# Splitting -log f into two float32r halves, and joining y to the next chunk's scores, from the third block on

## The chip, the cores and the metric

The kernel runs on one core of a Trainium2 chip. Times are device microseconds (us), given as the median of several runs.

## The reference, cut to what matters

```python
f = 1.0 / (1.0 + np.exp(-f_logit))               # q, k, v, f_logit: (4, 8, 768, 48)
for t in range(S):
    state = f[:, :, t, :, None] * state + np.einsum('bhd,bhe->bhde', k[:, :, t], v[:, :, t])
    y[:, :, t] = np.einsum('bhd,bhde->bhe', q[:, :, t], state)
# y is reshaped to x: 3072 tokens x 384
h = x @ w_in                                     # 384 -> 2048
sp = np.maximum(h, 0.0) + np.log1p(np.exp(-np.abs(h)))
out = (h * erf(sp)) @ w_out                      # 2048 -> 384
```

All arithmetic is float32. The first part is a recurrence over 768 steps, the second a pair of large products around an elementwise function.

## The kernel before

The recurrence is done in 24 chunks of 128 tokens, three chunks to a block, eight blocks. A chunk `g` goes through four stages, and each needs the one before it:

- `stage_d`: `tri` times -log f gives the running sums `ps_d`. ScalarE makes two exponentials of them, `dp` and `kd`. VectorE makes `qd`, GpSimd multiplies into `kd`.
- `stage_t`: TensorE transposes `qd` and `kd`, the copies are `qT` and `kT`.
- `stage_s`: scores `sc` on TensorE, masked into `A` on VectorE, then `dS` and the state `Mbd`.
- `stage_y`: `y` from `A`, v and the state, ScalarE copies it into `xT`.

```python
def prepare(blk, j0, j1):                 # -log f of a whole block, in place
    ...
    nc.vector.tensor_scalar(out=lt, in0=lt, scalar1=LOGIT_MIN, scalar2=None, op0=ALU.max)
    use_exp_ln()
    nc.scalar.activation(out=lt, in_=lt, func=AF.Exp, scale=-1.0)
    nc.scalar.activation(out=lt, in_=lt, func=AF.Ln, bias=1.0)

def stage_d(g):
    ...
    nc.tensor.matmul(ps, lhsT=tri[:], rhs=lts[blk][:, j, :], start=True, stop=True)
    ...    # dp and kd on ScalarE, qd on VectorE, kd on GpSimd
```

These stages are laid by hand between the large products. A *slot* is one large product, of 384 columns: two passes of 0.32 us, so about 0.64 us. Iteration `it` runs the hidden products of block `it` and the projections of block `it-2`, 96 slots together (48 in the first two iterations, which have no projection). The chunk stages of block `it+1` are dropped in at evenly spaced slots, and with them go activation steps of finished groups, clamps, and, up to about 146 us, unpacking of the weights on VectorE.

```python
todo = deque(stages(blk) if blk < n_blocks else [])
at = [int(3 + (n - 13) / max(1, len(todo)) * i) for i in range(len(todo))]
for s, _ in enumerate(slots(it)):         # one large product
    ...                                   # due weight steps
    if at and s == at[0]:
        at.pop(0)
        f, g = todo.popleft()
        f(g)
        ...
    ...                                   # step: is an activation step due at s?
    if step and not 66 <= s < 72:
        act_step()
    if it + 2 < n_blocks and s == (16 if it < 2 else n // 2):
        prepare(it + 2, 0, CPB)
```

The position of a stage thus depends on how many stages there are: `at` spaces them evenly. The order in which this loop emits instructions is the order in which ScalarE and VectorE run them in the traces looked at below. The large products take turns in a pool of two buffers (`hps` and `ops`); VectorE copies `hps` out to `Hg` from the third block on, ScalarE copies `ops` out to `osb`.

## Time and profile before

| | before |
|---|---|
| time, median of 4 (range) | 648.12 us (648.04 to 648.44) |
| span of the profiled execution | 646.4 us |
| hidden products of block 0 / 3 / 7 begin at | 32.19 / 208.86 / 515.28 us |
| busy in that span: TensorE, VectorE, ScalarE | 630.7, 474.6, 510.0 us |

Read the third row as marks: where a block's hidden products begin tells how late the kernel is at that point, and two kernels can be compared mark by mark. (Blocks are counted from 0: block 3 is the fourth.) The lines that carry the reading are shown in the prediction.

### The profile page before, as it was taken

The page shows a single profiled execution, that of the slowest core. Times are in us where ns is not written, and L with a number is a line of the kernel's source. Part 1 is how long each engine was busy: PE and PEld are TensorE (multiplying, and loading weights), DVE is VectorE, ACT ScalarE, POOL GpSimd, SP SyncE. Part 2 cuts the span into 40 slices and gives each one's busy share as a digit, 9 for nine tenths or more (in the row PEclk, how much of TensorE's full clock was granted, in tenths as well). Part 3 has the DMA queues.
Part 4 walks back from the last instruction along what each step waited for, and adds up shares of the span by engine and source line. Part 5 has one row for each costly group of instructions (what it writes and reads, how often), then busy time and mean ns, then how long its engine had stood idle before and what let it go on. Part 6 is the DMA issues. An engine that isn't in the chain of part 4 may idle for free.

```text
span 646.4 us, 9360 instructions
## 1 busy us (share of the span) xinstructions
PE 630.7 (98%) x3815; PEld 393.8 (61%) x3815; DVE 474.6 (73%) x440; ACT 510.0 (79%) x459; POOL 59.1 (9%) x61
## 2 busy tenths in 40 slices
PE   8899999999999999999999999999999999999995
PEld 6756666665656666656656666666666655555553
DVE  4798889997777886678657687668765686577761
ACT  5446667679899888797898978978787899799971
POOL 0112101120110010201210002201020000000000
PEclk9999999999999999999999999999999999999999
DMA  9996872310113120221203211020001000000001
GB/s 192 252 269 149 220 204 50 75 24 14 37 37 74 25 38 13 62 50 25 38 13 76 45 28 24 13 75 1 1 0 38 1 0 1 37 1 0 37 1 41
DMA packets 120689, 36.90 MB, mean 57 GB/s; under 512 B 112448, under 2 KB 115520, under 8 KB 120640
## 3 DMA queue, kind: packets, MB, share of 16 engines
q1 hardware_dynamic: 118560, 35.84, 24.0%
q10 hardware_dynamic: 2080, 0.39, 0.4%
q8 instruction: 32, 0.52, 0.3%
q14 instruction: 17, 0.14, 0.1%
HBM read 31.46 MB, written 4.72 MB: 56 GB/s over the span
## 4 chain that ended last, share of the span: by engine, by line
PE 75%; ACT 12%; DVE 8%; issue 3%; DMA 1%; POOL 0%; DVEq 0%; POOLq 0%; ACTq 0%
PE hps L491 32%; PE ops L524 27%; PE y L147 5%; ACT x L153 5%; PE sc L375 4%; DVE e L158 3%; PE ps_t L357 3%; PE ps_d L330 2%; ACT yl L446 1%; ACT e L457 1%; PE dS L403 1%; ACT L297 1%; ACT e L442 1%; ACT L457 1%; DVE Hg L460 1%
## 5 line engine op out<-in xcount | busy, mean ns | idle before, releaser
L491 PE MATMUL hps<-xT,w_in_sb 128*128 128x384 f32 x768 | 259.9, 490 | 1.3 <-ACT xT L432 0.6
L524 PE MATMUL ops<-w_out_sb,Hg 128*128 128x384 f32 x768 | 256.2, 489 | 1.2 <-DVE Hg L460 1.2
L158 DVE SCALAR_TENSOR_TENSOR e<-x,e 128x1536 f32<-128x1536 f32 x128 | 230.3, 1799 | 6.3 <-DVE e L158 0.5
L153 ACT ACTIVATE x<-yl,serf_bias 128x1536 f32<-128x1536 f32 x128 | 195.0, 1566 | 14.1 <-DVE e L158 14.0
L524 PEld LDWEIGHTS ops<-w_out_sb,Hg 128*128 128x128 f32 x768 | 143.7, 190 | 99.4 <-issue 2.2
L491 PEld LDWEIGHTS hps<-xT,w_in_sb 128*128 128x128 f32 x768 | 142.5, 190 | 96.9 <-issue 2.2
L460 DVE TENSOR_TENSOR Hg<-Hg,e 128x1536 f32<-128x1536 f32 x32 | 56.5, 1765 | 63.9 <-ACT e L457 63.8
L503 DVE COPY Hg<-hps 128x768 f32<-128x768 f32 x48 | 45.7, 952 | 20.1 <-PE hps L491 19.7
L347 POOL TENSOR_TENSOR kd<-kn,kd 128x384 f32<-128x384 f32 x21 | 29.4, 1401 | 323.1 <-issue 185.7
L457 ACT ACTIVATE e<-e 128x1536 f32<-128x1536 f32 x32 | 47.5, 1483 | 10.6 <-DVE e L158 10.3
L446 ACT ACTIVATE yl<-e 128x1536 f32<-128x1536 f32 x32 | 47.5, 1485 | 0.4
L442 ACT ACTIVATE e<-Hg 128x1536 f32<-128x1536 f32 x32 | 47.3, 1477 | 0.0
L343 DVE TENSOR_TENSOR qd<-qn,dp 128x384 f32<-128x384 f32 x24 | 14.2, 591 | 36.6 <-ACT dp L333 36.6
L297 ACT ACT_TABLE_LOAD x31 | 39.8, 1283 | 1.3 <-PEq L929 0.8
L457 ACT ACT_TABLE_LOAD x31 | 39.8, 1283 | 0.5
L419 POOL TENSOR_TENSOR Mbd<-Sn,Tall 48x192 f32<-48x192 f32 x32 | 28.6, 893 | 97.0 <-DVE Sn L416 82.3
L389 DVE TENSOR_TENSOR A<-sc,tri 128x1024 f32<-128x1024 f32 x24 | 29.3, 1219 | 8.4 <-PE sc L375 8.1
L147 PE MATMUL y<-A,vt 128*32 128x128 f32 x768 | 35.2, 277 | 0.1
L147 PEld LDWEIGHTS y<-A,vt 128*32 128x32 f32 x768 | 27.4, 109 | 12.0 <-issue 4.1
L432 ACT COPY xT<-y 128x384 f32<-128x384 f32 x24 | 11.3, 472 | 26.0 <-PE y L147 25.9
L375 PEld LDWEIGHTS sc<-qT,kT 48*128 48x128 f32 x384 | 23.3, 187 | 12.5 <-issue 11.3
L147 PE MATMUL y<-qT,Mbd 128*32 128x128 f32 x480 | 30.2, 273 | 0.0
(72 smaller groups left out, 389.9 us busy)
## 6 DMA issues: line engine op xcount, KB each, us to landing
lt<-in_f_logit_dram SPq DMA_DIRECT2D x24, 192.0 KB, 4.2
qn<-in_q_dram SPq DMA_DIRECT2D x24, 192.0 KB, 3.2
Hg<-in_moe_w_out_dram SPq DMA_DIRECT2D x6, 768.0 KB, 6.3
kn<-in_k_dram SPq DMA_DIRECT2D x23, 192.0 KB, 3.2
vt<-in_v_dram SPq DMA_DIRECT2D x23, 192.0 KB, 3.1
w_out_sb<-in_moe_w_in_dram SPq DMA_DIRECT2D x4, 768.0 KB, 6.3
Hg<-in_moe_w_in_dram SPq DMA_DIRECT2D x4, 768.0 KB, 7.1
out_dram<-osb SPq DMA_DIRECT2D x8, 384.0 KB, 2.5
```

The lines of the kernel that those rows point to most:

```text
L147: nc.tensor.matmul(y[M * i : M * (i + 1), kt, :], lhsT=terms[n][0], rhs=terms[n][1], start=(n == 0), stop=(n == len(terms) - 1), skip_grou ...
L153: nc.scalar.activation(out=dst[:], in_=y[:], func=AF.Square, bias=serf_bias[:, i : i + 1], scale=SERF_K)
L158: nc.vector.scalar_tensor_tensor(out=e[:], in0=x[:], scalar=SERF_AB[i][1], in1=e[:], op0=ALU.add, op1=ALU.mult)
L297: nc.scalar.add_instruction(mybir.InstLoadActFuncSet(act_func_set_id=EXP_LN, name=nc.get_next_instruction_name(), engine=mybir.EngineType. ...
L375: nc.tensor.matmul(sc[:, r, a, :], lhsT=kT[rows(r), a, :], rhs=qT[rows(r), a, :], start=True, stop=True,)
L442: nc.scalar.activation(out=e[:], in_=h, func=AF.Exp)
L446: nc.scalar.activation(out=y[:], in_=e[:], func=AF.Ln, scale=SERF_C, bias=1.0)
L457: nc.scalar.activation(out=e[:], in_=e[:], func=AF.Tanh)
L460: nc.vector.tensor_tensor(out=h, in0=h, in1=e[:], op=ALU.mult)
L491: nc.tensor.matmul(hps[:, j, 0:TB], lhsT=w_in_sb[:, kt, ft * P : (ft + 1) * P], rhs=xTs[blk][:, kt, :], start=(kt == 0), stop=(kt == n_k - 1),
L503: nc.vector.tensor_copy(out=to, in_=hps[:, :, 0:TB])
L524: nc.tensor.matmul(ops[tt // 2][:, tt % 2, 0:d_model], lhsT=gr["h"][:, j, tt * P : (tt + 1) * P], rhs=w_out_sb[:, ft, :], start=(ft == 0), ...
```

## The change

The intent has two parts. A float32 product appears as two passes. If -log f is split into an upper part, cast to the type float32r, and what is left of it, two float32r products can add up to the same sum, each meant to take one pass. And `y` of a chunk directly followed by `sc` and `dS` of the next saves TensorE one return to full tiles. Since the split needs a place in the order, `stages` is rewritten too. The core of the diff, with cuts:

```diff
+    SPLIT = 2 * CPB + 1                                # from chunk 7 on
...
+    def stage_split(g):
...
+        split[g] = work1.tile([P, 2, d_model], FP32R, name="split", tag="kT")
+        upper, lower = split[g][:, 0, :], split[g][:, 1, :]
+        nc.vector.tensor_copy(out=upper, in_=lt)
+        nc.vector.tensor_tensor(out=lower, in0=lt, in1=upper.bitcast(FP32), op=ALU.subtract)
...
-        nc.tensor.matmul(ps, lhsT=tri[:], rhs=lts[blk][:, j, :], start=True, stop=True)
+        if g < SPLIT:
+            nc.tensor.matmul(ps, lhsT=tri, rhs=lts[blk][:, j, :], start=True, stop=True)
+        else:
+            both = split.pop(g)
+            for n in range(2):
+                nc.tensor.matmul(
+                    ps, lhsT=tri_r[:], rhs=both[:, n, :], start=(n == 0), stop=(n == 1)
+                )
...
+    def stage_y_s(g):
+        stage_y(g)
+        stage_s(g + 1)
...
-            todo = []
             if blk == 1:
                 todo = [(stage_d, g0), (stage_t, g0)]
+                for g in range(g0, g0 + CPB):
+                    todo += [(stage_d, g + 1), (stage_s, g), (stage_t, g + 1), (stage_y, g)]
+                return todo
+            todo = [(stage_s, g0)] if blk == 2 else []
             for g in range(g0, g0 + CPB):
-                last = g == n_chunks - 1
-                todo += [] if last else [(stage_d, g + 1)]
-                todo += [(stage_s, g)]
-                todo += [] if last else [(stage_t, g + 1)]
-                todo += [(stage_y, g)]
+                if g < n_chunks - 1:
+                    todo += [(stage_split, g + 1)] if g + 1 >= SPLIT else []
+                    todo += [(stage_d, g + 1), (stage_t, g + 1), (stage_y_s, g)]
+                else:
+                    todo += [(stage_y, g)]
```

The buffer `Sn` is dropped (the state is updated in place), and `tri` is written as float32r.

More of the change, by code (lines that the diff above doesn't have):

```diff
@@ L39 @@
 FP32 = mybir.dt.float32
+FP32R = mybir.dt.float32r
 I32 = mybir.dt.int32
@@ L110 @@
     ident = fixed("ident", [P, P])
-    tri = fixed("tri", [P, P])
+    tri_r = fixed("tri", [P, P], FP32R)
+    tri = tri_r[:].bitcast(FP32)
     w_in_sb = fixed("w_in_sb", [P, n_k, d_ff])
@@ L312, in prepare @@
         nc.scalar.activation(out=lt, in_=lt, func=AF.Ln, bias=1.0)
+    split = {}
+    def stage_split(g):
+        blk, j = divmod(g, CPB)
+        lt = lts[blk][:, j, :]
+        split[g] = work1.tile([P, 2, d_model], FP32R, name="split", tag="kT")
+        upper, lower = split[g][:, 0, :], split[g][:, 1, :]
+        nc.vector.tensor_copy(out=upper, in_=lt)
+        nc.vector.tensor_tensor(out=lower, in0=lt, in1=upper.bitcast(FP32), op=ALU.subtract)
     totals = {}
@@ L319, in keep_busy @@
         for _ in range(n):
-            nc.tensor.matmul(busy[-1], lhsT=tri[:], rhs=tri[:], start=True, stop=True)
+            nc.tensor.matmul(busy[-1], lhsT=tri, rhs=tri, start=True, stop=True)
     def stage_d(g):
@@ L391, in stage_s @@
             in0=sc[:].rearrange("s r a t -> s (r a) t"),
-            in1=tri[:].unsqueeze(1).broadcast_to((P, H, P)),
+            in1=tri.unsqueeze(1).broadcast_to((P, H, P)),
             op=ALU.mult,
@@ L407, in stage_s @@
         new, old = Mbds[g % 2], Mbds[(g + 1) % 2]
-        Sn = work1.tile([P, HP, D], FP32, name="Sn", tag="Sn")
         for r in range(2):
@@ L416, in stage_s @@
             nc.vector.tensor_tensor(
-                out=Sn[rows(r)], in0=dS[rows(r)], in1=old[rows(r), :, r, :], op=ALU.add
+                out=new[rows(r), :, r, :], in0=dS[rows(r)], in1=old[rows(r), :, r, :], op=ALU.add
             )
             nc.gpsimd.tensor_tensor(
-                out=new[rows(r), :, r, :], in0=Sn[rows(r)], in1=total, op=ALU.mult
+                out=new[rows(r), :, r, :], in0=new[rows(r), :, r, :], in1=total, op=ALU.mult
             )
@@ L585 @@
             load_f(g)
-        nc.gpsimd.memset(tri[:], 1.0)
+        nc.gpsimd.memset(ident[:], 1.0)
         nc.gpsimd.affine_select(
-            out=tri[:], in_=tri[:], pattern=[[1, P]], compare_op=ALU.is_ge, fill=0.0,
+            out=ident[:], in_=ident[:], pattern=[[1, P]], compare_op=ALU.is_ge, fill=0.0,
             base=0, channel_multiplier=-1,
         )
+        nc.gpsimd.tensor_copy(out=tri_r[:], in_=ident[:])
         make_identity(nc, ident)
@@ L709 @@
                     f(g)
-                    if f is stage_y:
+                    if f in (stage_y, stage_y_s):
                         load_to(g + LOOK)
```

## The prediction

> **What bounds the kernel now.** I read the busy shares first, then the instructions of TensorE in order of time, then each engine by stage, then who waits for whom. The page and the table of groups by line and form (columns: busy us, mean ns of one, idle before) give:
>
> ```profile
> PE 630.7 (98%) x3815; PEld 393.8 (61%) x3815; DVE 474.6 (73%) x440; ACT 510.0 (79%) x459; POOL 59.1 (9%) x61
> ...
> L330 PE MATMUL ps_d<-lt,tri 128*128 128x384 f32 x48 | 19.5, 488 | 0.1
> ```
>
> 98% alone would not prove a bound, because matmuls overlap. The timeline does (start, duration, instruction group): one group begins where the one before leaves off.
>
> ```profile
> 352.27 13.17 PE L491 MATMUL hps<-xT,w_in_sb 128*128 128x384 f32 x40
> 365.28 0.81 PE L330 MATMUL ps_d<-lt,tri 128*128 128x384 f32 x2
> 365.92 4.03 PE L491 MATMUL hps<-xT,w_in_sb 128*128 128x384 f32 x12
> ...
> 376.96 4.68 PE L491 MATMUL hps<-xT,w_in_sb 128*128 128x384 f32 x14
> 381.57 1.10 PE L147 MATMUL y<-A,vt 128*32 128x128 f32 x32
> 382.61 4.78 PE L524 MATMUL ops<-w_out_sb,Hg 128*128 128x384 f32 x14
> 387.23 0.81 PE L330 MATMUL ps_d<-lt,tri 128*128 128x384 f32 x2
> 387.87 4.68 PE L524 MATMUL ops<-w_out_sb,Hg 128*128 128x384 f32 x14
> 392.48 1.16 PE L375 MATMUL sc<-qT,kT 48*128 48x128 f32 x16
> 393.57 0.56 PE L403 MATMUL dS<-vt,kd 128*48 128x48 f32 x16
> ```
>
> Read the starts, not the durations. One float32 product of 384 columns appears as two rows; 365.92 - 365.28 = 0.64 us for both, 0.32 each. No step has an idle bracket, so here TensorE is the bound and every nanosecond taken from it counts.
>
> By stage (columns: stretch, its length, then busy us and instructions of PE, PEld, DVE, ACT, POOL; granted clock, DMA share, GB/s) it is not the same everywhere:
>
> ```profile
> 85.00:146.00 61.00, 59.22 (x438) 37.22 (x436) 58.20 (x67) 40.66 (x46) 10.77 (x10) 1.00 0.34 69
> 146.00:223.00 77.00, 76.60 (x467) 47.39 (x468) 59.37 (x47) 70.22 (x61) 7.02 (x5) 1.00 0.19 39
> 223.00:300.00 77.00, 77.00 (x466) 47.81 (x465) 54.63 (x46) 66.23 (x57) 7.85 (x9) 1.00 0.19 39
> 300.00:377.00 77.00, 77.00 (x473) 47.87 (x472) 54.42 (x44) 63.33 (x55) 7.04 (x5) 1.00 0.19 39
> ```
>
> From 85 to 146 us VectorE is busy 58.20 of 61: it still unpacks weights there. The four waits of TensorE in the early stages (view of waits, 80 to 210 us) are for it, or for ScalarE just behind it:
>
> ```profile
> PE ps_t L357 <- DVE Sn L416: 0.9, 1, 0.9
> PE ps_t L357 <- DVE Mbd L412: 0.6, 1, 0.6
> PE hps L491 <- ACT osb L531: 0.4, 1, 0.4
> PE hps L491 <- DVE Hg L503: 0.3, 1, 0.3
> ```
>
> So there are two regimes: up to about 190 us VectorE and ScalarE decide, or very nearly; from 190 to 562 us TensorE alone. The last 84 us look like ScalarE's in the chain, but ScalarE starts that last run only after waiting for TensorE:
>
> ```profile
> 562.03 0.48 ACT L536 COPY osb<-ops 128x384 f32<-128x384 f32 x1 [1.78 <-PE ops L524]
> ```
>
> A gain made by TensorE before 562 us therefore moves the whole tail.
>
> **What the Trainium skill says.** (1) "FP8 and Floating Point Precision", section TensorE Precision Notes: the array's native precision is about FP22, a reduced reading of float32 exists, and true float32 takes four passes. The trace agrees as far as it can: two rows per product at 0.32 us each, whereas 384 columns at the 2.4 GHz of the page "TensorE: Matmul & The Clock Gate" (section Back-to-back issue gap) would be about 0.16 us; so four column times. No run so far shows a float32r product. (2) "TensorEngine Tiling (Array Packing)", section Key Properties: a change of tiling mode drains the array. The trace agrees, and sizes it, below. (3) The clock page, section LDWEIGHTS: a weight load costs its columns at 1.2 GHz, 107 ns for 128. The single instructions of the trace start 104 to 109 ns apart where loads follow one another, so a load hides under a product of 160 ns.
>
> **The change part by part.**
>
> Product of -log f. Old: 2 x 0.322 = 0.645 us (starts above). New: two single passes; estimate by (1) 2 x 0.163 = 0.325. Removes 0.32 us from each of 17 chunks (7 to 23): 5.4 us.
>
> Order. Old, per chunk: full products, y, full products, sc, dS, full products. New: y, sc, dS as one burst, so one return to full tiles and one departure fewer. Size: 14 full passes cost 14 x 0.322 = 4.51 us, but 382.61 to 387.23, just after y, is 4.62, and 387.87 to 392.48, just before sc, is 4.61. Each edge costs 0.10 to 0.11 us; y-to-sc keeps a drain of its own, as y-to-full had. Saving 0.2 us in each of 17 joins (y of 6 to 22): 3.4 us. Full sum on TensorE: 8.8 us, 1.4%.
>
> VectorE pays for the split: one copy and one subtraction of 128x384. A one-input operation of that shape took 0.36 us (the clamp of lt), a two-input one 0.59 (qd). About 0.95 us each chunk, 16 us altogether. From 190 us on its windows show over 20 us idle in 77, three splits per window fit, and it lies beside TensorE. In 85 to 146 us there are three splits, 2.8 us, on an engine with 2.8 us idle: nothing is left over. Dropping Sn for an in-place update costs nothing; it lengthens no chain that TensorE waits for.
>
> Lead times. Formerly about two slots lay between ps_d and the transposes, some 11 us in the middle of the kernel; now one, 7 products or 4.5 us, and only 2 or 3 products (1.3 to 1.9 us) before 146 us. The transpose of kd needs ScalarE's two exponentials (0.97) and GpSimd's product (1.40): 2.6 us with signalling, plus ScalarE's lag. In the trace before, kd was done 2.7 to 3.6 us after the start of ps_d in the typical chunk, but 7.3 for chunk 12 and 6.2 for chunk 18. So I expect some new waits "ps_t for kd": about 0.5 us each early, and a few of about 1 us later, where ScalarE lags over 2 us.
>
> Sum. Up to 190 us the gains of TensorE (about 2.6 us) are swallowed because VectorE or ScalarE ends last, and the three splits push that end out by about 2 us, roughly the 2.8 less what the idle takes. After 190 us: 11 products x 0.32 + 12 joins x 0.2 = 5.9 us gained, less about 0.5 us of new waits. Net 5.4 - 2 = 3.4, and some chance that the early stage absorbs its extra better than I charge: I say 4.1 us. 648.1 - 4.1 = 644.0 us.
>
> **Rivals.**
>
> A: everything counts. TensorE never waits for the split, 8.8 us come off: 639.3. For it: the lags of VectorE behind TensorE at kT and qd are under 1.6 us everywhere in the trace, and 1.5 us or more of lead is given to the split. Against it: no idle time of VectorE in 85 to 146 us.
>
> B: float32r runs no faster than a float32 row, 0.32 us per product, or a change between the two kinds drains the array as a change of tiles does. Then 5.4 us fall away or shrink to about 2, and the joins alone are left after 190 us (12 x 0.2 = 2.4), less the early 2: 647 to 648. For it: nothing in this trace shows float32r. Against: the transposes, another kind, follow the full products in the trace with no edge.
>
> C: the shorter lead makes TensorE wait for kd in most chunks, about 1 us x 17: the gain is eaten, 648 to 652. For it: chunks 12 and 18. Against: ScalarE's lag at ps_d was 1.2 us or less in most of the other chunks, and 4.5 us of lead less 2.6 leaves 1.9, plus the 0.4 of the first four transposes.
>
> **Range and chances.** 644.0 lies between A and B; A at its full size and C at its worst are the ends. 640.5 to 647.5 holds it 8 times in 10, with B just beyond. A gain of over 2% needs 13 us, more than the largest sum (8.8): chance 0.02. A loss of over 2% would need a wait of over a microsecond in every chunk on top of all gains lost: 0.01. Within 2%: 0.97.
>
> **What would show it.** The two ps_d rows starting about 0.16 us apart rather than 0.32 (step 1; if 0.32, B). The burst y, sc, dS without full products between, and stretches of full products with two edges fewer per chunk (step 2). Split rows of about 0.36 and 0.59 us on VectorE, and VectorE at over 95% in the stage that ends near 146 us; the start of the fourth block's hidden products (hps; 208.9 us before) not earlier, perhaps 1 to 2 us later, then a lead growing by about 1.5 us per block (step 3). Waits "ps_t for kd" new, small early and rare later; if they sum to over 4 us, C is right. If the lead at 208.9 us is already 3 us, my claim that the early stage swallows the gain is wrong. If it grows by less than 1 us per block, a term of TensorE's own sum is wrong.

## The result, and the profile after

The changed kernel took 656.52 us (656.26 to 656.70, 4 runs) beside 648.12 us for the kernel before: 8.4 us slower, a ratio of 1.0127 with a 95% interval of 1.0112 to 1.0142. The forecast was 4.1 us faster. Here and below a ratio is the mean time of one kernel's runs over that of the other's in the same rounds, so it isn't quite the ratio of the medians quoted.

The page of the changed kernel, busy times:

```profile
PE 627.5 (96%) x3815; PEld 395.9 (60%) x3815; DVE 490.4 (75%) x474; ACT 510.3 (78%) x459; POOL 66.5 (10%) x62
```

TensorE has less work than before (627.5 us against 630.7) in a longer span (654.8 us against 646.4). The time went into waits. Where, the marks tell: the hidden products of block 0, 3 and 7 now begin at 32.61, 222.13 and 523.51 us.

Up to block 3 the kernel before needs 208.86 - 32.19 = 176.67 us, the changed one 222.13 - 32.61 = 189.52. In the joined order 1.58 us of small products (`sc` and `dS` of chunk 12: 1.09 + 0.49) have moved ahead of that mark, so the delay is 189.52 - 176.67 - 1.58 = **11.3 us**. From block 3 to block 7 the changed kernel needs 301.38 us against 306.42; 1.58 us of that moved out, so the gain there is **3.5 us**. With the start, 0.4 us later, that is 11.3 - 3.5 + 0.4 = 8.2 of the 8.4 us. All the loss is early.

By stage (columns as in the prediction), the first and the last of the windows shown there:

```profile
85.00:146.00 61.00, 52.58 (x405) 32.91 (x405) 50.24 (x64) 32.26 (x39) 8.54 (x9) 0.94 0.26 54
...
300.00:377.00 77.00, 77.00 (x477) 48.83 (x476) 58.32 (x52) 66.20 (x57) 7.02 (x5) 1.00 0.19 39
```

The first row refutes the expected picture at once. From 85 to 146 us VectorE was to be over 95% busy; it is busy *less* than before, 50.24 us for 58.20, TensorE too, and the granted clock is 0.94. No engine is busy throughout here: they wait for each other in a ring. TensorE's waits from 80 to 210 us (us in total, times, longest):

```profile
PE ps_t L378 <- DVE qd L364: 5.0, 2, 3.9
PE ps_d L349 <- DVE split L325: 1.9, 3, 1.2
PE hps L516 <- ACT osb L556: 1.6, 1, 1.6
PE ps_t L378 <- POOL kd L368: 1.3, 1, 1.3
PE hps L516 <- DVE Hg L528: 0.9, 1, 0.9
```

10.7 us, where the kernel before had 2.2. The largest, 3.9 us for `qd` of chunk 8, is worth following back. In the kernel before, TensorE and ScalarE pass the same place like this:

```profile
97.75 0.81 PE L330 MATMUL ps_d<-lt,tri 128*128 128x384 f32 x2
...
104.05 0.60 PE L357 MATMUL ps_t<-ident,qd 128*128 128x128 f32 x4
```
```profile
98.60 0.49 ACT L333 ACTIVATE dp<-ps_d 128x384 f32<-128x384 f32 x1 [0.80 <-PE ps_d L330]
...
102.06 1.17 ACT L311 ACTIVATE lt<-lt 128x1152 f32<-128x1152 f32 x1 [2.59 <-DVE lt L307]
```

There 6.3 us lie between the product and the transposes, and ScalarE does `dp` of this chunk *before* it turns to the next block's -log f. ScalarE of the changed kernel:

```profile
97.95 0.48 ACT L452 COPY xT<-y 128x384 f32<-128x384 f32 x1 [0.17 <-PE y L149]
104.65 1.16 ACT L314 ACTIVATE lt<-lt 128x1152 f32<-128x1152 f32 x1 [6.22 <-DVE lt L310]
...
108.38 0.49 ACT L354 ACTIVATE dp<-ps_d 128x384 f32<-128x384 f32 x1
```

`dp` of chunk 8 now stands *behind* the exponential of the clamped block. That exponential waits 6.22 us with the engine idle, and what it waits for is VectorE's clamp (source line 310), which comes late in VectorE's own queue:

```profile
101.94 1.15 DVE L275 SCALAR_TENSOR_TENSOR w_out_sb<-w_out_sb 128x768 uint32<-128x768 uint32 x1
103.01 0.35 DVE L325 CAST split<-lt 128x384 fp32r<-128x384 f32 x1
...
103.86 0.75 DVE L310 TENSOR_SCALAR lt<-lt 128x1152 f32<-128x1152 f32 x1
...
119.31 1.22 DVE L410 TENSOR_TENSOR A<-sc,tri 128x1024 f32<-128x1024 f32 x1 [5.32 <-PE sc L396]
```

So the product, begun at 103.50, was there by 104.5 us, but `dp` could not start before 108.4, after the two activations of 1.16 us and two operations more. `kd` was done 8.5 us after the start of its product, where the kernel before took 2.8 for this chunk. TensorE pays:

```profile
109.61 1.09 PE L378 MATMUL ps_t<-ident,qd 128*128 128x128 f32 x4 [3.87 <-DVE qd L364]
112.04 1.12 PE L378 MATMUL ps_t<-ident,kd 128*128 128x128 f32 x4 [1.34 <-POOL kd L368]
112.94 3.53 PE L516 MATMUL hps<-xT,w_in_sb 128*128 128x384 f32 x6
```

Two waits, 5.2 us, and then six full passes take 3.53 us instead of about 2: from 109.0 to 115.8 us the granted clock is 0.50, and the first five of these passes start 0.64 us apart. Last, the ring closes: the scores come behind the stalled transposes, and VectorE, the engine that was to be full, stands idle for them for 5.32 us (119.31 above).

All of this was in the program's order and could have been read without a run. The order of ScalarE's instructions in the two built kernels (chunk 8's exponentials marked):

```
before                                   after
Activation x<-yl,serf_bias               Activation x<-yl,serf_bias
Activation dp_104<-ps_d      (chunk 8)   TensorCopy xT<-y
Activation kd_102<-ps_d      (chunk 8)   Activation lt<-lt            (needs the clamp)
Activation lt<-lt  (needs the clamp)     Activation lt<-lt
Activation lt<-lt                        TensorCopy Hg_114<-hps
TensorCopy Hg_114<-hps                   Activation w_out_sb<-Hg_115
Activation w_out_sb<-Hg_115              Activation dp_104<-ps_d      (chunk 8)
TensorCopy qT<-ps_t                      Activation kd_102<-ps_d      (chunk 8)
```

The reason is arithmetic of slots. In the iteration of 48 slots the old list has 12 stages, spaced 35/12 slots: `ps_d` of chunk 8 at slot 14, its transposes at slot 20. The new list has 13, spaced 35/13: split at 16, `ps_d` at 19, transposes at 21. The clamp stays at slot 16. Nobody moved it; the stages moved past it.

Late, the gain is there as predicted. TensorE:

```profile
299.55 4.68 PE L516 MATMUL hps<-xT,w_in_sb 128*128 128x384 f32 x14
303.77 0.80 PE L349 MATMUL ps_d<-split,tri 128*128 128x384 f32 x2
304.42 4.68 PE L516 MATMUL hps<-xT,w_in_sb 128*128 128x384 f32 x14
```

The two `ps_d` rows start 0.47 us apart here, not 0.16 as the prediction asked for. But the first start lies before the pass ahead of it has ended, so count across the group: from 299.55 to 304.42 is 4.87 us, less 14 passes of 0.322 leaves 0.36 us for both products, where the old one took 0.645. A block from mark to mark (4 to 5) takes 373.13 - 297.62 = 75.51 us where it took 362.70 - 285.70 = 77.00: 1.49 us for three chunks, 0.50 each. Two kernels of the next section have one part alone: `split_only` takes 76.10 us there and `order_only` 76.41, so 0.30 is the product and 0.20 the join. Eleven chunks between marks 3 and 7 should give 5.5 us; 3.5 arrived. The difference is one wait for the output copy at 430.87 us, on ScalarE again:

```profile
425.00 0.49 ACT L354 ACTIVATE dp<-ps_d 128x384 f32<-128x384 f32 x1 [1.62 <-PE ps_d L349]
...
427.18 1.48 ACT L482 ACTIVATE e<-e 128x1536 f32<-128x1536 f32 x1
428.57 1.56 ACT L155 ACTIVATE x<-yl,serf_bias 128x1536 f32<-128x1536 f32 x1
430.03 0.78 ACT L556 COPY osb<-ops 128x768 f32<-128x768 f32 x1
```
```profile
430.87 0.91 PE L516 MATMUL hps<-xT,w_in_sb 128*128 128x384 f32 x2 [2.04 <-ACT osb L556]
```

`dp` waits for the product's new, later slot; two activation steps that come behind `dp` in the order run late; and the copy that frees TensorE's buffer comes behind those.

Early, the product brought nothing. The first four pairs of float32r products take 1.59, 0.91, 2.15 and 1.23 us from pass to pass; the other 13 take 0.35. This is chunk 8's:

```profile
99.40 4.14 PE L516 MATMUL hps<-xT,w_in_sb 128*128 128x384 f32 x12
103.50 0.95 PE L349 MATMUL ps_d<-split,tri 128*128 128x384 f32 x2
104.28 1.45 PE L516 MATMUL hps<-xT,w_in_sb 128*128 128x384 f32 x4
```

VectorE finishes the two halves of chunk 8 at 103.36 and 103.95, and the two products start at 103.50 and 104.00: each just after its half. Over four times the 0.35, these pairs lose 4.5 us. The list of waits shows 1.9 of it; the rest is hidden, because the profile draws a TensorE row longer than it keeps the next one waiting (103.50 + 0.95 lies past 104.28).

### The profile page after: what moved, and what is told of

Same layout as the page of the kernel before. It is cut to its first block, busy times and chain, and to the rows that moved or that the text cites. A ratio compares the mean times of both kernels' runs of the same rounds, so it can differ in the third digit from the quotient of the medians.

```text
span 654.8 us, 9382 instructions
## 1 busy us (share of the span) xinstructions
PE 627.5 (96%) x3815; PEld 395.9 (60%) x3815; DVE 490.4 (75%) x474; ACT 510.3 (78%) x459; POOL 66.5 (10%) x62
## 4 chain that ended last, share of the span: by engine, by line
PE 70%; ACT 13%; DVE 11%; issue 4%; POOL 1%; DVEq 0%; ACTq 0%; POOLq 0%
PE hps L516 29%; PE ops L549 25%; ACT x L155 5%; DVE e L160 5%; PE y L149 5%; PE sc L396 4%; PE ps_t L378 3%; ACT e L482 2%; ACT yl L471 1%; ACT L482 1%; PE dS L424 1%; DVE Hg L485 1%; ACT e L467 1%; ACT L300 1%; PE ps_d L334 1%
## 5 line engine op out<-in xcount | busy, mean ns | idle before, releaser
L549 PE MATMUL ops<-w_out_sb,Hg 128*128 128x384 f32 x768 | 253.5, 487 | 1.3 <-DVE Hg L485 1.3
L368 POOL TENSOR_TENSOR kd<-kn,kd 128x384 f32<-128x384 f32 x21 | 34.8, 1659 | 252.2 <-ACT kd L357 148.5
L439 POOL TENSOR_TENSOR Mbd<-Mbd,Tall 48x192 f32<-48x192 f32 x32 | 30.2, 943 | 172.3 <-DVE Mbd L436 137.2
L354 ACT ACTIVATE dp<-ps_d 128x384 f32<-128x384 f32 x24 | 11.7, 490 | 21.7 <-PE ps_d L349 13.8
```

Source lines behind the costliest of these rows:

```text
L368: (nc.vector if blk == 0 else nc.gpsimd).tensor_tensor(out=kd, in0=kns[g % NQ][:].rearrange("t (h d) -> t h d", d=D), in1=kd, op=ALU.mult)
L549: nc.tensor.matmul(ops[tt // 2][:, tt % 2, 0:d_model], lhsT=gr["h"][:, j, tt * P : (tt + 1) * P], rhs=w_out_sb[:, ft, :], start=(ft == 0), ...
```

## The experiments

Two theories stood at the start. A: the order costs the time, because chunk 8's exponentials fall behind the clamp on ScalarE (A1 in the expectations) or because the lead between `ps_d` and the transposes is short. B: the split costs it, as work on a full VectorE. All eighteen kernels gave correct results, and the diffs are against the changed kernel unless said. The delay up to block 3 and the change from block 3 to 7 are worked out as above, from the one profiled execution of each; the start of block 0 alone differs by up to 1 us from kernel to kernel, so differences under about 1 us mean nothing, and a stretch of half clock, which some executions have and others not, adds 1.7 us or more (see from_fourth).

### Parting the change

**order_only**: the new order without the split.

```diff
     def stage_split(g):
+        return
...
-        if g < SPLIT:
+        if True:
```

> The new order from the third block on, but the product of -log f stays one float32 product and the split does nothing (its slot stays empty). Theory A (the loss of about 10 us between 85 and 146 us comes from the order: in the third block only 2 or 3 products lie between ps_d, the transposes and the scores, so TensorE waits, and VectorE, full of weight work, then idles behind it): the early loss stays, the gain later shrinks from 0.5 to 0.2 us a chunk, so 656 to 660 us. Theory B (the loss comes from the split's 2.8 us on a full VectorE): the early loss goes, 645 to 648 us.

Measured: 657.72 us (657.14 to 658.17), ratio 1.0141 [1.0124, 1.0158]. The delay up to block 3 is 8.7 us, with the same waits for `qd` (5.3 us) and `kd` (1.4). The order alone is as slow as the whole change: A, not B. Late it loses 1.5 us where the joins should gain 2.2: 2.0 us in the wait for the output copy and 1.7 in a half clock after it.

**split_only**: the old order, the split of chunk g+2 made after `y` of chunk g, in a buffer of `A`'s pool instead of `kT`'s.

```diff
-                    todo += [(stage_d, g + 1), (stage_s, g), (stage_t, g + 1), (stage_y, g)]
+                    todo += [(stage_d, g + 1), (stage_s, g), (stage_t, g + 1), (stage_y_split, g)]
... (the same for the later blocks; stage_y_split is stage_y, then stage_split(g + 2))
```

> The two float32r products from chunk 7 on, in the old order (split placed with y, in the buffer of A). Theory A: the early loss is at most the split's own 2 to 3 us; after 190 us 11 chunks gain 0.3 us each: 645 to 649 us. Theory B: the early loss is still near 10 us: 653 us or more.

Measured: 647.89 us (647.46 to 648.07), ratio 0.9990 [0.9974, 1.0007]. Early it loses 1.3 us, late it gains 2.0. The float32r products are no loss, but the 17 x 0.3 = 5.1 us that they take off TensorE do not arrive either.

**from_fourth**: the third block keeps the old order and the old product.

```diff
-    SPLIT = 2 * CPB + 1
+    SPLIT = 3 * CPB + 1
...
+            if blk == 2:
+                ...                        # the old list
+                return todo
-            todo = [(stage_s, g0)] if blk == 2 else []
+            todo = [(stage_s, g0)] if blk == 3 else []
```

> Both parts, but from the fourth block on, when the weights are unpacked. Theory A and theory B both: the early loss goes; 14 chunks gain 0.5 us (7 us), less one or two waits of 2 us for the copy of the output: 641.5 to 645 us. If it stays above 650, the loss is in neither the early stage's order nor its split.

Measured: 649.86 us (649.64 to 650.48), ratio 1.0022 [1.0005, 1.0038]. A miss: 6.7 us of the 8.4 go away, but no gain appears. Its first block in the new order has waits for `kd` of 2.6 us, and late it meets the output copy again, with a tail:

```profile
423.38 0.91 PE L516 MATMUL hps<-xT,w_in_sb 128*128 128x384 f32 x2 [2.04 <-ACT osb L556]
```
```profile
421.02:424.43 3.41, 1.37 (x6) 0.74 (x6) 0.00 (x0) 2.68 (x4) 0.00 (x0) 1.00 0.06 16
424.43:427.84 3.41, 3.41 (x11) 2.43 (x10) 2.07 (x2) 2.92 (x3) 0.00 (x0) 0.50 1.01 259
```

After a wait of 2.04 us the clock is granted at 0.50 for 3.41 us, which costs 1.7 us more. In the changed kernel the same wait at 430.87 us has no such tail:

```profile
426.42:429.83 3.41, 2.41 (x8) 1.13 (x6) 0.00 (x0) 3.40 (x3) 0.58 (x1) 1.00 0.08 1
429.83:433.24 3.41, 2.37 (x13) 1.80 (x14) 0.55 (x1) 2.35 (x5) 0.00 (x0) 1.00 0.43 158
```

The traces show the difference. In the clock records of all twenty, the granted clock is 1.00 or 0.50 and changes only on a grid of 3.41 us, whose offset differs between executions. In from_fourth the whole wait fell into one window of the grid; in the changed kernel it was shared, 1.00 us idle in one window and 1.04 in the next. Laid over all twenty traces (from 45 us on, whole windows at full clock), the grid gives 12 windows in which TensorE was idle 1.96 us or more, and each is followed by half clock. Of 3472 windows with 1.91 us idle or less only one is (wide_pool, 1.70 us). So a wait of 2 us costs 2 or 3.7 here, by where it falls on that execution's grid.

**prepare_late**: the changed kernel with one number changed. The clamp goes to slot 22 of the second iteration, behind `stage_d` and `stage_t` of chunk 8.

```diff
-                if it + 2 < n_blocks and s == (16 if it < 2 else n // 2):
+                if it + 2 < n_blocks and s == (16 if it == 0 else 22 if it == 1 else n // 2):
```

> The changed kernel, with the log of the fourth block's gates prepared 6 slots later in the stage near 100 us, so that ScalarE does not take it ahead of chunk 8's exponentials. Theory A1 (within A: the longest wait, 3.9 us for qd of chunk 8, is ScalarE held 6.2 us behind VectorE's clamp): that wait and the 1.3 us for kd behind it and the slow clock after it go, 649.5 to 653 us. If the short lead alone does it, whatever stands in ScalarE's queue: 655 to 657 us.

Measured: 651.18 us (651.04 to 652.48), ratio 1.0049 [1.0032, 1.0066], as A1 expected. The delay up to block 3 falls from 11.3 to 5.7 us. The clamp's place alone is worth 5.6 us; 2.4 of it is the half clock after the wait, which this profile does not have.

### Is the rest the short lead?

**wide**: the joined order and the split, but every `ps_d` and transpose at its old slot (the empty place keeps the count), the split early.

```diff
+                todo += [] if last else [(stage_d, g + 1)]
+                todo += [(nothing, g)] if merged else [(stage_s, g)]
+                todo += [] if last else [(stage_t, g + 1)]
+                todo += [(stage_y, g)] if last or blk < 2 else [(stage_y_s, g)]
... (merged: from chunk 7 on; stage_y_s also makes the split of chunk g + 2; SPLIT = 2 * CPB + 2)
```

> Both parts from the third block on (the split from chunk 8), but ps_d, the transposes and y keep the slots that they have in the kernel before, two slots apart; only the scores move, up to the y ahead of them. If the short lead between ps_d, transposes and scores is what cost 10 us early and the stall of ScalarE at the output copies later (theory A), no new wait stays but the split's own on VectorE before 146 us (0 to 3 us), and 17 joins of 0.2 us and 16 products of 0.3 us are gained in part or whole: 640.5 to 645 us. If joining the scores to y is itself harmful early: 650 us or more.

Measured: 654.08 us (653.19 to 654.55), ratio 1.0087 [1.0070, 1.0104]: a clear miss. Here the exponentials of chunk 8 come ahead of the clamp again and the lead is the old one, yet the delay up to block 3 is 6.6 us. VectorE is full to the end of the weights:

```profile
146.82 3.54 PE L521 MATMUL hps<-xT,w_in_sb 128*128 128x384 f32 x6 [3.50 <-DVE Hg L533]
```

TensorE waits 3.5 us for a copy of VectorE, and a half clock of 3.41 us follows. It also waits 2.8 us for `qT` of chunk 8: VectorE's clamp is late, and now it is `qT` that stands behind the clamped block on ScalarE. The short lead is not the sole cause of the rest; the next runs ask whether the split's work on VectorE is another.

**wide_fourth**: the same from the fourth block on (`blk < 3`, `SPLIT = 3 * CPB + 2`).

```diff
-    SPLIT = 2 * CPB + 2
+    SPLIT = 3 * CPB + 2
-                merged = blk > 2 or blk == 2 and g > g0
+                merged = blk > 3 or blk == 3 and g > g0
```

(against wide)

> The same with the old slots, but both parts only from the fourth block on. Theory A: the 2.2 us wait for the output copy in the middle of the sixth block that every kernel with the new slots shows is gone, and so is the slow clock after it: 641 to 643.5 us, 6 us or more below the same start with the new slots (649.9). If that wait is not from the slots, 645 us or more.

Measured: 646.96 us (646.58 to 649.62, 6 runs), ratio 0.9986 [0.9969, 1.0004]. The early delay is gone (0.3 us); late it gains 1.8 us only, and the wait for the output copy (1.7 us) remained. A miss of 3.5 us.

**wide_split_fourth**: the joined order from the third block, the split from the fourth.

```diff
-    SPLIT = 2 * CPB + 2
+    SPLIT = 3 * CPB + 2
```

(against wide)

> Old slots; the scores joined to y from the third block on, the split and its products only from chunk 11 on. Against the kernel with both from the third block it says what three splits cost or gain on the full VectorE before 146 us: theory A has them near neutral (their 0.9 us each of VectorE against 0.3 us each of TensorE), so this one is the same or up to 2 us faster: 640 to 643.5 us.

Measured: 648.93 us (648.71 to 651.25, 6 runs), ratio 1.0017 [1.0002, 1.0032]. Slower than expected, but 5.2 us faster than wide, from which it differs only in three early splits (and their products). Delay up to block 3: 2.5 us, against 6.6. So three splits, 0.9 us each, cost about 4 us where VectorE is full, 1.7 of it in wide's half clock.

**wide_twice**: wide, with each split from chunk 13 on done twice, the same values again.

```diff
-        nc.vector.tensor_copy(out=upper, in_=lt)
-        nc.vector.tensor_tensor(out=lower, in0=lt, in1=upper.bitcast(FP32), op=ALU.subtract)
+        for _ in range(2 if g > 12 else 1):
+            nc.vector.tensor_copy(out=upper, in_=lt)
+            nc.vector.tensor_tensor(out=lower, in0=lt, in1=upper.bitcast(FP32), op=ALU.subtract)
```

> Old slots, both parts from the third block, with the copy and the subtraction of the split each done twice from chunk 13 on: 11 x 0.9 = 10 us more of VectorE's work after 190 us. If VectorE's time is hidden there, as the prediction has it, within 1 us of the kernel that does them once; if it is not, up to 10 us slower.

Measured: 659.33 us (656.89 to 660.20), ratio 1.0157 [1.0134, 1.0181], 5 us more than wide for 11 x 0.9 = 10 us of added work on VectorE. TensorE's waits from 200 to 560 us, wide and then wide_twice:

```profile
PE hps L521 <- ACT osb L561: 2.1, 2, 1.7
PE hps L521 <- DVE Hg L533: 1.2, 3, 0.5
```
```profile
PE hps L522 <- DVE Hg L534: 4.3, 4, 1.5
PE hps L522 <- ACT osb L562: 3.3, 2, 2.7
```

In this profile 3.1 us are lost to a half clock after the longest of these waits. So the doubled split does not lie beside TensorE's work: 20 us idle in 77 is an average, and at the copies of `hps` the engine has less. The single split did fit in the changed kernel: from block 3 to block 7 its only wait is the one for the output copy, and order_only has that without any split.

### The clamp again, and another engine for the split

**order_clamp_late** is order_only with the edit of prepare_late:

```diff
+        return                             # in stage_split, with `if True:` in stage_d
-                if it + 2 < n_blocks and s == (16 if it < 2 else n // 2):
+                if it + 2 < n_blocks and s == (16 if it == 0 else 22 if it == 1 else n // 2):
```

> The order alone, in its new slots (657.7 us), with the clamp and log of the fourth block's gates 6 slots later. If ScalarE held behind that clamp is a cost of the order and not of the split, this falls by about as much as the changed kernel did (656.5 to 651.2): 651.5 to 653.5 us. If it needs the split on VectorE to hurt, 656 us or more.

Measured: 651.59 us (651.10 to 655.04), ratio 1.0058 [1.0026, 1.0090]; a hit. Delay up to block 3: 2.4 us, from 8.7. The clamp's place is worth 6.3 us here (2.7 of it half clock), 5.6 with the splits.

**wide_clamp_late** is wide_split_fourth with the same edit:

```diff
-                if it + 2 < n_blocks and s == (16 if it < 2 else n // 2):
+                if it + 2 < n_blocks and s == (16 if it == 0 else 22 if it == 1 else n // 2):
```

> The scores joined to y from the third block on, old slots, splits from chunk 11 on (648.9 us), with the clamp 6 slots later. In that kernel TensorE waits 2.3 us for qT of chunk 8, which stands behind the clamped log on ScalarE. If the clamp is all of the early loss left, the wait goes and the time is 646.3 to 647.2 us, that of the same kernel joined from the fourth block only (647.0). If VectorE's full queue is what counts, 648 us or more.

Measured: 649.25 us (648.16 to 650.49), ratio 1.0014 [0.9988, 1.0041]; no difference from wide_split_fourth. The delay up to block 3 falls from 2.5 to 1.7 us only: a wait for `qT` went away, and waits for `xT` (1.3 us) and for VectorE's copy of `hps` (2.0) took its place. With the exponentials ahead of it, the clamp isn't what costs.

**split_pool** and **wide_pool** are split_only and wide_fourth with the split on GpSimd:

```diff
-        nc.vector.tensor_copy(out=upper, in_=lt)
-        nc.vector.tensor_tensor(out=lower, in0=lt, in1=upper.bitcast(FP32), op=ALU.subtract)
+        nc.gpsimd.tensor_copy(out=upper, in_=lt)
+        nc.gpsimd.tensor_tensor(out=lower, in0=lt, in1=upper.bitcast(FP32), op=ALU.subtract)
```

> The old order with the two float32r products from chunk 7 on (647.9 us), the split done on GpSimd (about 10% busy) instead of VectorE. If VectorE's 0.9 us a chunk is what ate the gain of 17 x 0.3 us, the early delay of 1.3 us and the later waits shrink: 644 to 646 us. If GpSimd is too slow for its lead of one slot, waits for the split appear: 649 us or more.

Measured: 647.49 us (647.04 to 650.08, 6 runs), ratio 0.9989 [0.9968, 1.0011]. Expected was 644 to 646. No more than split_only.

> Both parts from the fourth block on in the old slots (647.0 us), the split on GpSimd. If the later waits for the copy of the hidden products (1.6 us) and of the output (2.6 us) come from VectorE's extra 0.9 us a chunk, they shrink: 642.5 to 645 us. If they come from the scores standing ahead on VectorE and ScalarE, 646.5 to 647.5 us.

Measured: 656.71 us (656.29 to 657.83), ratio 1.0127 [1.0102, 1.0152], 10 us slower than with VectorE. GpSimd's timeline in wide_pool says why:

```profile
314.73 2.48 POOL L439 TENSOR_TENSOR Mbd<-Mbd,Tall 48x192 f32<-48x192 f32 x2 [16.18 <-DVE Mbd L436]
317.27 1.91 POOL L325 CAST split<-lt 128x384 fp32r<-128x384 f32 x1
319.26 0.99 POOL L326 TENSOR_TENSOR split<-lt,split 128x384 fp32r<-128x384 f32 x1
```

In the joined order the scores' state update (2.48 us) stands ahead of the split in GpSimd's queue, and then the copy takes 1.91 us where VectorE takes 0.35. (Of the 13 copies in this kernel the quickest took 0.50 us; no run here shows why the others are slower.) TensorE's waits for the two halves sum to 5.0 and 4.1 us in this kernel. In split_pool, where the split follows `y` and comes ahead of the next state update, they sum to 1.6.

### The output copy late

Is the late loss the place of an activation step ahead of the output copy? The **hold** kernels keep four more slots free of activation steps, in the sixth iteration only:

```diff
-                if step and not 66 <= s < 72:
+                if step and not (62 if it == 5 else 66) <= s < 72:
```

> Both parts from the fourth block on in the new slots (649.9 us), with ScalarE's step of the activation at slot 65 of the sixth block put behind the copy of the output. If the 2.0 us wait for that copy and the slow clock after it are this step standing ahead of the copy, both go: 646 to 648 us. If ScalarE is simply full there, the wait stays or moves: 649 to 650.5 us.

Measured: 646.89 us (646.63 to 649.39), ratio 0.9987 [0.9965, 1.0008], 3 us less than from_fourth: a hit. The wait for the copy is gone. But of the waits from 380 us to the end one grew, from 1.2 us:

```profile
PE ops L549 <- DVE Hg L485: 2.6, 1, 2.6
```

It is the last wait of the kernel, for the last activation, which now comes a step later.

> The same step moved, in the kernel with both parts from the fourth block on in the old slots (647.0 us), where the wait for the copy is 1.7 us. If it is the step's place: 644.8 to 645.8 us, and the best kernel of the study. If ScalarE is full: 646.5 to 647.5 us.

Measured: 647.85 us (646.12 to 653.34, 6 runs), ratio 0.9997 [0.9965, 1.0029]. No gain and a wide spread: again 2.6 us at the end, and a slow clock in some runs.

> Control: the same step moved in the kernel before, where TensorE waits only 0.1 us for that copy. Both theories: 647.6 to 648.6 us, no change; if it is faster by 1 us or more, the gain of the other two is not a recovered wait.

Measured (the kernel before with this one edit): 650.45 us (649.24 to 651.78), ratio 1.0035 [1.0014, 1.0057]. Not unchanged, as expected, but 2 us slower, with the same 2.6 us at the end. A step left out must be given back.

The **moved** kernels give it back, at slot 72:

```diff
-                if step and not 66 <= s < 72:
+                if step and not (62 if it == 5 else 66) <= s < 72:
                     act_step()
+                    if it == 5 and s == 72:
+                        act_step()
```

> Both parts from the fourth block on in the old slots (647.0 us); ScalarE's step of slot 65 of the sixth block is moved behind the copy of the output and made up at slot 72, so that no later activation slips. The wait for the copy (1.7 us) should go and the last wait of the kernel stay at 1.2 us: 644.8 to 646 us, faster than both kernels. If the step's loss was not what raised the last wait to 2.6 us, 647 to 648 us as without the make-up.

Measured: **645.14 us** (644.55 to 645.77, 6 runs), ratio 0.9946 [0.9933, 0.9959]. A hit, and the fastest kernel, 3 us below the kernel before.

> The same make-up in the new slots from the fourth block on (649.9 us as it was, 646.9 with the step merely held). Without the longer last wait (2.6 to 1.2 us): 645 to 646 us. If the make-up stands in another copy's way, 646.5 us or more.

Measured: 645.86 us (645.20 to 648.08, 6 runs), ratio 0.9953 [0.9940, 0.9966]; a hit, 4 us below from_fourth.

> The changed kernel with two edits of order only: the fourth block's clamp 6 slots later (651.2 us by itself) and the step at slot 65 of the sixth block moved to slot 72. If these two places in ScalarE's queue are the largest terms, 648.5 to 649.5 us, and what is left against the full sum of 639 is the split's and the scores' load on the full VectorE before 146 us (5.6 us of delay at 209 us with the clamp moved). If 650.5 or more, another late wait is left.

Measured: 649.81 us (649.63 to 650.03), ratio 1.0017 [1.0001, 1.0033], 1.4 us below prepare_late and just above what was expected. Waits for `qd` (3.2 us), for the split (2.1) and for an output copy at 197 us (1.6) remain: the third block is still in the new order. In this profile the 2.08 us wait at 107.41 fell into one window of the clock's grid, so the delay up to block 3 is 7.3 us, not the 5.7 of prepare_late.

The page of the best kernel:

```profile
PE 625.1 (97%) x3815; PEld 394.2 (61%) x3815; DVE 487.7 (76%) x466; ACT 509.3 (79%) x459; POOL 52.3 (8%) x62
```

TensorE's work is 5.6 us below that of the kernel before; the span, 643.0 us, is 3.4 below. It should have saved 13 x 0.5 = 6.5 us (chunks 11 to 23). Its mark of block 7 is 3.4 us earlier than before. Its listed waits up to there are 1.8 us more than before; that leaves about 1.3 us that no wait explains.

### The delays side by side

| kernel | joined from | split from | clamp ahead of chunk 8's exponentials | delay up to block 3 | block 3 to 7 |
|---|---|---|---|---|---|
| after | third block | chunk 7 | yes | +11.3 | -3.5 |
| order_only | third | none | yes | +8.7 | +1.5 |
| prepare_late | third | chunk 7 | no | +5.7 | -3.5 |
| order_clamp_late | third | none | no | +2.4 | +1.5 |
| split_only | none | chunk 7 | no | +1.3 | -2.0 |
| wide_split_fourth | third, old leads | chunk 11 | no | +2.5 | -1.8 |
| wide | third, old leads | chunk 8 | no | +6.6 | -1.8 |
| wide_fourth | fourth, old leads | chunk 11 | no | +0.3 | -1.8 |
| wide_fourth_moved | fourth, old leads | chunk 11 | no | +0.3 | -3.7 |

Differences in the first four rows part the 11.3 us: 5.6 to 6.3 for the clamp's place, 2.6 to 3.3 for the splits on a full VectorE, 2.4 for the rest of the order. The first contains the half clock after the wait: `after`, `order_only` and `wide` lost 2.4, 2.7 and 1.7 us of their early delay to it, the other rows nothing, and the `+1.5` of the two order kernels contains 1.7. The causes do not simply add: early splits cost 1.3 us in the old order and about 4 in wide.

## Why the prediction was wrong

**What bounds the kernel.** Right for the late part, and the reading of two regimes too. But for the early part the prediction asked only which engine is *busy*, and went on to add up work there. From 85 to 146 us TensorE (59.22 of 61 us) and VectorE (58.20) pass work to each other, and there a change of order alone, with no work added, cost 8.7 us.

**The product.** Right for 13 of 17 chunks: 0.36 us for both in place of 0.645, so 0.29 saved where 0.32 was predicted. The first four waited for their halves and saved nothing. Rival B is refuted: split_only gains the 0.30 per chunk without any join.

**The join.** Right: 0.20 us per chunk, in order_only by itself.

**VectorE's cost.** The sizes were right (0.35 and 0.56 us). Late, "three splits per window fit, and it lies beside TensorE" held for the changed kernel, but with less room than 20 us idle in 77 suggests: the doubled split cost about 5 us for 10 of work, in waits for VectorE's copies of `hps` and for ScalarE's output copy, and in a half clock.

**The early stage.** The prediction charged this stage with "the three splits push that end out by about 2 us". It came 11.3 us late. The term of 2 us stood for the splits alone; they cost 2.6 to 3.3, near enough. What was missing altogether is the order: 5.6 to 6.3 us because the stages moved past the clamp on ScalarE's queue, and 2.4 us more. The step that failed is the prediction's lead time, the waits that shorter leads would bring: "about 0.5 us each early". It took ScalarE's lag from the order before ("kd was done 2.7 to 3.6 us after the start of ps_d") into the new one, where it was 8.5 us for chunk 8. ScalarE stood idle for 6.22 us because the head of its queue waited for VectorE; and when that was released, with the product of chunk 8 there too, it first ran the four operations that stood ahead of chunk 8's exponentials. The Trainium skill says this much ("TensorE: Matmul & The Clock Gate", section "Architectural detail: the array is 16× 32×32, not 1× 128×128": ScalarE's and VectorE's queues are strict first-in, first-out), and the trace agrees with its 6.22 us; the prediction did not use that statement, nor compare the two programs' orders on ScalarE, where the exchange stands in plain sight.

Even the expected sign, VectorE over 95% busy up to 146 us, came out reversed (82%). The prediction's alternative, that the stage would absorb more than it charged, was the wrong side to hedge.

**The clock.** The prediction had no term for it. From 109.0 to 115.8 us TensorE ran at half clock; it was busy for 4.88 of these 6.83 us, so 2.4 us were lost. Together with 8.5 us of added waits and the 2.5 us hidden in the first four float32r pairs that makes 13.4. TensorE's work up to block 3 should also have shrunk by six chunks at 0.5, so some 14.3 us had to be lost; about 1 us of it is in no wait listed.

**The late part.** "About 0.5 us of new waits" was 2.0 us, one wait, for an output copy behind activation steps on ScalarE. That this is its cause is shown: moving the step takes 1.4 to 4 us off (1.7 of the 4 is from_fourth's half clock). The tail did move with TensorE.

**Rival C** gave a slower kernel (648 to 652) for a wrong reason: waits for `kd` in most chunks. Its number doesn't follow from its own terms either: 17 waits of 1 us less the full gain of 8.8 is 8.2 us slower, 656.3. That this lies beside the measured 656.5 is luck. (Its reading of the trace also passed over chunks 5 and 21, whose `kd` was done 5.0 and 5.6 us after the start of the product.) One wait for `kd`, of 1.3 us, is in the whole kernel; the lead that fell short was that of `qd`, by the way of ScalarE's queue.

What stays open: about 1 us of the early loss; in part, why the order costs 2.4 us even with the clamp late (order_clamp_late waits 2.8 us for `qd` and 1.7 for copies out of the large products' buffers, 4.5 against 2.2 before; about 1 us is in no wait); and 1.3 us in the best kernel.

## What to carry to other kernels

In a hand-laid schedule, a change of order must be checked engine by engine on the built program: for each in-order queue, what now stands ahead of what, and what that head waits for. Idle time as an average is no slack; ask for it at the places where another engine waits. And be wary of starting a change in the stage where two engines are already full: starting one block later turned the same change, with one activation step moved (from_fourth_moved), from 8.4 us slower into 2.5 us faster by the medians.

## What the Trainium skill lacked or had wrong

- "FP8 and Floating Point Precision", TensorE Precision Notes: it names a reduced reading of float32 but no rate. Here two float32r products of 384 columns take 0.36 us together, where a true float32 product takes 0.645.
- "TensorEngine Tiling (Array Packing)", Key Properties: the drain on a change of mode has no size. Here each edge costs 0.10 to 0.11 us, and joining y to the scores saves 0.2 us per chunk.
- "TensorE: Matmul & The Clock Gate", section "Why this matters for your kernels": it advises against idle gaps over about 3 us. Here a wait of 2.04 us (from_fourth, 423 us) was followed by 3.41 us at a granted clock of 0.50, while the same 2.04 us in the changed kernel (431 us) was not. The advised limit was too generous here: 12 of 12 windows of 3.41 us with 1.96 us or more idle were followed by half clock.
- No page says how to find a head-of-line wait before a run, by comparing the order of each engine's instructions in two built programs. Here one such exchange cost 5.6 to 6.3 us.
